# Nine r·k tiles transposed by DMA, smaller load groups and a new instruction order in an RWKV-6 plus mixture-of-adapters kernel

## The chip, the cores and the metric

One core of a Trainium2 chip runs the whole kernel. The metric is the device time of one execution in microseconds (us). Three runs of the kernel before gave 92.51, 93.12 and 93.5 us, so the median is 93.12 us.

## What is computed

The inputs are r, k, v, w of shape (4, 8, 768, 48), that is 4 batches, 8 heads, 768 steps and 48 channels. A linear-attention recurrence runs over the steps, and its output goes through a top-2 mixture of eight rank-16 adapters:

```python
for t in range(S):                       # attention, per batch and head
    y[t]  = r[t] @ (state + (u * k[t]) v[t]^T)
    state = w[t][:, None] * state + k[t] v[t]^T
x = y as (B*S, H*D)                      # 3072 rows of 384
logits = x @ w_gate                      # 8 experts, top 2, softmax over these two
out = x + sum over the two of  weight * ((x @ A[e]) @ B[e])
```

## The kernel before

**Tiling.** The 3072 rows are 24 tiles of 128 rows (6 tiles to a batch), and each tile is 128 rows by 384 columns (8 heads of 48). All steps of a tile t are small functions named `step(t)`, written `step.t` in the order list.

**Steps of one tile.** `load_w`, `load_rk`, `load_v` bring the inputs in: w by SyncE's (SP's) hardware DMA queue, r, k and v by GpSimd's (POOL's) software queue, which casts to 16 bits on the way. `ln` takes the logarithm of w for two tiles on ScalarE (ACT). `cs` and `ci` sum it up along the rows by matmuls, and `grow` and `exps` take exponentials of that on ACT. `mult` scales r and k with them (VectorE, DVE), `tr` transposes both on TensorE (PE), `trev` copies the result out of PSUM, `amm` multiplies r with k, `aev` masks the product on DVE, `kv` and `sev` update the state, `ymm` makes y. The diagonal term with u needs r·k: `rkp` multiplies r and k elementwise (POOL or DVE) into the half of a buffer that `mult` of the tile before has just read, so `rkp.t` waits for `mult.(t-1)`. `xk.(t)` then transposes in one PSUM tile both the finished rows `xs` of tile t (three 128x128 blocks) and the r·k of tile t+3 (`LEAD` = 3, three more blocks). `xkev` copies the six blocks to SBUF. From the r·k blocks `dgmm` makes the diagonal factors (three tiny matmuls), `dgev` copies those of two tiles, `dv` multiplies them with v on POOL, and `xev` adds them to y on DVE: `xs`.

**Adapters.** `lgmm`, `gate`, `gmax`, `gsel`, `gmul` make the gate in batches of (4, 4, 4, 4, 4, 3, 1) tiles; `zmm`, `zw`, `zT`, `zTev` the low-rank part; `dmm` its second product; `oev` adds x and leaves the output rows in `res`, either on DVE, or on ACT with one extra PE matmul by the identity that adds x in PSUM; `store` issues the output on SP.

**What sets the order.** A written-out list `ORDER` names every step once. Each engine executes its own steps in the sequence of this list, and waits on semaphores where it needs another engine or a DMA. Two steps on different engines are not tied to each other by their place in the list. The strings in `ENGINES` choose the engine for each tile (A for ACT, D for DVE, P for POOL). Each DMA waits, besides its data, for the landing of the DMA eight before it on its queue.

Lines that matter below: L174 `load_w`, L192 `load_rk`, L200 `load_v`, L337 `mult`, L345 `rkp`, L350 `dgmm`, L362 `dv`, L390 `tr`, L414 `aev`, L458 `xev`, L467 the transposes of `xk`, L273 copies on ACT (`trev`, `xkev`, `zTev`), L282 `ln`, L480 `lgmm`, L524 `zmm`, L572 and L573 `dmm` (identity matmul and product), L591 and L593 `oev` on ACT and on DVE, L600 `store`.

Of the kernel before, what the change touches and what calls it, by code (L numbers as in the profile page):

```python
# [37 lines left out]
ORDER = """
warm.0 warm.1 csc.0 warm.2 warm.3 warm.4 load_w1.0 warm.5 load_v.0 ln.0 load_rk.2 load_rk.3 load_v.2 cs.0 rkp.0 ci.0
xk.-3 grow.0 multr.0 exps.0 xkev.-3 trr.0 ln1.0 trevr.0 load_w.2 masks.0 load_rkf.1 load_wsb.0 mult.0 adapters.0  # L40
load_rk.4 load_w.4 tr.0 trev.0 pad.0 cs.1 amm.0 load_w.6 grow.1 ci.1 exps.1 load_rk.6 load_w.8 aev.0 kv.0 load_v.4
sev.0 ln.2 pad.1 cs.2 grow.2 rkp.1 load_rk.8 mult.1 xk.-2 xkev.-2 rkp.2 ci.2 load_v.8 tr.1 exps.2 cs.3 kv.1 cast16.0
mult.2 load_rk.12 grow.3 trev.1 dgmm.0 dgmm.1 dgev.1 sev.1 ymm.0 rkp.3 casts.0 amm.1 load_v.12 load_w.10 tr.2 ci.3
aev.1 trev.2 exps.3 kv.2 dv.0 amm.2 ymm.1 sev.2 xev.0 xk.-1 dv.1 ln.4 load_rk.16 mult.3 tr.3 xkev.-1 xev.1 kv.3 cs.4
trev.3 aev.2 load_v.16 xk.0 grow.4 dgmm.2 pad.2 ci.4 xkev.0 sev.3 rkp.4 amm.3 dgmm.3 load_w.12 exps.4 mult.4 xk.1
rkp.5 dgev.3 dv.2 dv.3 xkev.1 load_v.20 cs.5 ymm.2 lgmm.0 dgmm.4 aev.3 grow.5 xev.2 lgmm.1 tr.4 ci.5 ln.6 exps.5
ymm.3 trev.4 cs.6 xk.2 amm.4 mult.5 rkp.6 xev.3 xkev.2 grow.6 ci.6 xk.3 tr.5 dgmm.5 lgmm.2 ln.8 exps.6 trev.5 cs.7
xkev.3 grow.7 aev.4 lgmm.3 dgmm.6 zmm.3 ci.7 amm.5 gate.3 mult.6 rkp.7 tr.6 gmax.3 ln.10 dgev.5 dv.4 exps.7 aev.5
kv.4 cs.8 load_rk.20 gsel.3 mult.7 gmul.3 ymm.4 trev.6 sev.4 grow.8 amm.6 ci.8 xev.4 kv.6 ln.12 dv.5 exps.8 tr.7
sev.6 xk.4 trev.7 cs.9 zw.3 zT.3 ymm.5 kv.7 xkev.4 aev.6 lgmm.4 zTev.3 dmm.0 dmm.1 grow.9 ci.9 xev.5 dmm.2 mult.8  # L50
sev.7 oev.0 dgmm.7 rkp.8 amm.7 load_w.14 exps.9 cs.10 oev.1 dgev.7 tr.8 ymm.6 dv.6 oev.2 grow.10 xk.5 ln.14 dv.7
ci.10 exps.10 aev.7 xev.6 store.0 kv.8 ymm.7 rkp.9 trev.8 cs.11 xk.6 mult.9 sev.8 xkev.5 amm.8 kv.9 tr.9 lgmm.5
grow.11 xkev.6 load_w.16 mult.10 ci.11 dmm.3 dgmm.8 rkp.10 xev.7 aev.8 dgmm.9 lgmm.6 xk.7 trev.9 exps.11 dgev.9
sev.9 amm.9 cs.12 xkev.7 oev.3 rkp.11 tr.10 grow.12 aev.9 load_w.18 ymm.8 mult.11 trev.10 ci.12 lgmm.7 dgmm.10 dv.8
xev.8 gate.7 exps.12 ymm.9 kv.10 sev.10 dv.9 amm.10 tr.11 gmax.7 xk.8 ln.16 xkev.8 rkp.12 mult.12 cs.13 rkp.13
grow.13 gsel.7 xev.9 zmm.7 gmul.7 dgmm.11 lgmm.8 store.1 ci.13 xk.9 trev.11 exps.13 tr.12 xkev.9 aev.10 cs.14
dgev.11 trev.12 zw.7 grow.14 amm.11 zT.7 ymm.10 kv.12 mult.13 load_w.20 store.2 load_w.22 dgmm.12 ci.14 aev.11 dv.10
zTev.7 ln.18 dmm.4 ymm.11 exps.14 xev.10 xk.10 xkev.10 lgmm.9 cs.15 dv.11 sev.12 oev.4 xev.11 grow.15 amm.12 dmm.5
dgmm.13 dgev.13 rkp.14 tr.13 lgmm.10 dmm.6 mult.14 xk.11 aev.12 rkp.15 oev.5 dmm.7 trev.13 ci.15 xkev.11 amm.13
# [4 lines left out]
rkp.17 trev.16 xkev.13 oev.8 mult.17 amm.16 exps.18 sev.16 store.5 dmm.9 xk.14 cs.19 mult.18 oev.9 tr.17 rkp.18
xkev.14 ymm.15 grow.19 dgmm.16 ci.19 trev.17 dmm.10 exps.19 dgmm.17 tr.18 lgmm.13 aev.16 cs.20 kv.18 amm.17 xev.15
trev.18 rkp.19 grow.20 dgev.17 sev.18 xk.15 mult.19 ci.20 xkev.15 rkp.20 oev.10 aev.17 exps.20 dv.16 tr.19 ymm.16
lgmm.14 lgmm.15 cs.21 trev.19 xev.16 kv.19 gate.15 mult.20 grow.21 gmax.15 amm.18 xk.16 xkev.16 aev.18 dgmm.18 dv.17
dmm.11 oev.11 ci.21 exps.21 ymm.17 gsel.15 dgmm.19 sev.19 dgev.19 mult.21 zmm.15 cs.22 amm.19 kv.20 ymm.18 grow.22
sev.20 rkp.21 store.6 xev.17 gmul.15 ci.22 dv.18 store.7 xk.17 exps.22 xkev.17 zw.15 aev.19 tr.20 zT.15 xev.18 cs.23
lgmm.16 mult.22 dgmm.20 lgmm.17 trev.20 zTev.15 amm.20 dmm.12 grow.23 ci.23 xk.18 oev.12 aev.20 rkp.22 tr.21 dmm.13  # L70
store.8 store.9 ymm.19 xkev.18 trev.21 dgmm.21 exps.23 dgev.21 oev.13 dmm.14 amm.21 dv.19 tr.22 oev.14 xev.19 xk.19
xkev.19 mult.23 ymm.20 dmm.15 lgmm.18 lgmm.19 rkp.23 dv.20 aev.21 dgmm.22 trev.22 dv.21 ymm.21 tr.23 amm.22 gate.19
oev.15 store.10 trev.23 kv.21 xev.20 xk.20 gmax.19 zmm.19 xev.21 xk.21 sev.21 xkev.20 xkev.21 dgmm.23 gsel.19 aev.22
dgev.23 gmul.19 zw.19 dv.22 amm.23 kv.22 zT.19 ymm.22 store.11 sev.22 kv.23 lgmm.20 dv.23 lgmm.21 zTev.19 dmm.16
aev.23 xev.22 xk.22 oev.16 ymm.23 xev.23 xkev.22 lgmm.22 dmm.17 dmm.18 gate.22 zmm.22 oev.17 oev.18 gmax.22 xk.23
gsel.22 dmm.19 xkev.23 gmul.22 lgmm.23 zw.22 zmm.23 zT.22 oev.19 gate.23 store.12 zTev.22 gmax.23 dmm.20 gsel.23
zw.23 dmm.21 oev.20 oev.21 store.13 dmm.22 zT.23 store.14 zTev.23 oev.22 store.15 dmm.23 store.16 oev.23 store.17
store.18 store.19 store.20 store.21 store.22 oeva.23 store.23 storea.23
# [59 lines left out]
def kernel(  # L138
# [317 lines left out]
    def xev(t):  # L456
# [2 lines left out]
                             st[t]["y_ps"].rearrange("p a b -> p (a b)"))  # L459
        st[t]["xs"] = xs  # L460

    def xk(t):
        xk_ps = pp.tile([128, 6, 128], FP16, name="xk_ps", **slot("xk", t))
        for q, src in enumerate((st[t]["xs"] if t >= 0 else None, st[t + LEAD]["rkp"] if t + LEAD < NT else None)):
            if src is not None:
                for j in range(3):
                    nc.tensor.transpose(xk_ps[:, 3 * q + j, :], src[:, j * 128:(j + 1) * 128], ident16)  # L467
# [191 lines left out]
```

## Time and profile before

| | |
|---|---|
| runs | 92.51, 93.12, 93.5 us |
| profiled execution, time | 93.14 us |
| profiled execution, span from first to last instruction | 91.4 us |
| mean granted TensorE clock | 0.994 |
| ACT busy | 69.0 us (75%) |
| POOL busy | 50.3 us (55%) |
| software DMA queue (r, k, v) | 6.69 MB, 43.0% of 16 engines' span |
| hardware DMA queue of SP | 10.55 MB, 35.5% |

The span is what the profile sees; 1.7 us of the execution lie around it. The slices cut the span into 40 parts of 2.3 us, each digit being the busy share in tenths. A matmul is charged from its start to a modelled end, and matmuls overlap, so the distance between the starts of two neighbours tells what one costs the engine.

### The profile page before, as it was taken

The numbers are of one execution on the slowest core, as the hardware profiler recorded it, in microseconds if no ns is written. First come the engines' busy times: TensorE is split into PE (matmuls) and PEld (weight loads), VectorE is DVE, ScalarE is ACT, GpSimd is POOL, SyncE is SP. The second block draws the span as 40 slices with busy tenths as digits, with TensorE's granted clock in tenths as the row PEclk, the third lists the DMA queues.
The fourth block names the chain that finished last, engine by engine and source line by source line (L and its number), as shares of the span: only waits on it lengthen the run. The fifth ranks groups of instructions, "written<-read, shape, count | busy, mean of one in ns | idle before, by whom it ended". The sixth has DMA issues, their size and how long they took to land.

```text
span 91.4 us, 3313 instructions
## 1 busy us (share of the span) xinstructions
PE 79.3 (87%) x1335; PEld 59.1 (65%) x1335; DVE 76.9 (84%) x165; ACT 69.0 (75%) x164; POOL 50.3 (55%) x77
## 2 busy tenths in 40 slices
PE   5978868997999999999599999999999999979510
PEld 2435336875776867887467788787778878955200
DVE  5612898989999799999589999999999999976830
ACT  5237659998799979993998999998889868628210
POOL 6999357358029834976175833954649752532000
PEclk9999999999999999999999999999999999999997
DMA  1999999999999999999999999322201043105481
GB/s 29 317 215 266 267 272 261 261 264 275 274 249 217 208 213 204 245 260 263 272 277 273 262 254 266 103 86 86 93 31 55 7 173 126 55 4 186 159 296 48
DMA packets 13599, 17.53 MB, mean 192 GB/s; under 512 B 912, under 2 KB 13328, under 8 KB 13584
## 3 DMA queue, kind: packets, MB, share of 16 engines
q0 software_dynamic: 6128, 6.69, 43.0%
q1 hardware_dynamic: 7312, 10.55, 35.5%
q8 instruction: 10, 0.16, 0.7%
q10 hardware_dynamic: 144, 0.10, 0.3%
q14 instruction: 5, 0.04, 0.1%
HBM read 19.29 MB, written 4.72 MB: 263 GB/s over the span
## 4 chain that ended last, share of the span: by engine, by line
PE 47%; DMA 19%; DVE 14%; ACT 8%; issue 4%; SPq 2%; ACTq 0%; DVEq 0%
DMA w_in<-in_w_dram 10%; DMA rk_first<-in_rk_dram 9%; PE trp L390 8%; PE xk_ps L467 6%; PE a_ps L408 5%; DVE at L414 5%; PE d_ps L573 3%; PE y_ps L452 3%; PE z_ps L524 3%; DVE rk L337 3%; PE cs_ps L316 3%; PE s_ps L425 3%; DVE xs L458 2%; PE cs_ps L304 2%; PE cs_ps L305 2%
## 5 line engine op out<-in xcount | busy, mean ns | idle before, releaser
L414 DVE TENSOR_TENSOR at<-a_ps,strict 128x1024 f16<-128x1024 f32 x24 | 29.2, 1216 | 2.2 <-PE a_ps L408 2.2
L362 POOL TENSOR_TENSOR dv<-v,dg 128x384 f32<-128x384 f16 x24 | 20.2, 859 | 10.4 <-ACT dg L267 10.2
L345 POOL TENSOR_TENSOR e<-rk 128x384 f16<-128x384 f16 x15 | 14.0, 935 | 12.2 <-DVE rk L337 9.6
L309 ACT ACTIVATE e<-cs_ps 128x384 bf16<-128x384 f32 x24 | 11.9, 497 | 4.5 <-PE cs_ps L305 4.4
L273 ACT COPY rkT<-trp 128x512 f32<-128x512 f32 (+1 forms) x23 | 13.3, 578 | 1.7 <-PE trp L390 1.4
L390 PE MATMUL trp<-ident,rk 128*128 128x128 bf16 x184 | 14.1, 219 | 0.4 <-DVE rk L337 0.4
L458 DVE TENSOR_TENSOR xs<-dv,y_ps 128x384 f16<-128x384 f32 x24 | 13.1, 546 | 0.9 <-PE y_ps L452 0.4
L337 DVE TENSOR_TENSOR rk<-rk,e 128x768 bf16<-128x768 f16 x22 | 12.0, 554 | 1.4 <-ACT e L320 1.4
L273 ACT COPY xkT<-xk_ps 128x384 f32<-128x384 f32 (+1 forms) x23 | 10.3, 449 | 3.5 <-PE xk_ps L467 3.2
L320 ACT ACTIVATE e<-cs_ps 128x384 bf16<-128x384 f32 x23 | 11.4, 495 | 1.0 <-PE cs_ps L316 1.0
L390 PEld LDWEIGHTS <-rk 128*128 128x128 bf16 x184 | 10.9, 98 | 1.9 <-DVE rk L337 0.8
L282 ACT ACTIVATE logw<-w_in 128x768 f16<-128x768 f32 x11 | 9.3, 846 | 1.5 <-DMA w_in<-in_w_dram 1.5
L408 PE MATMUL a_ps<-rkT 48*128 48x128 bf16 x192 | 9.5, 218 | 0.6 <-DVE at L414 0.4
L267 ACT CAST S_sb<-s_ps 128x384 bf16<-128x384 f32 x19 | 9.3, 487 | 0.6 <-PE s_ps L425 0.4
L452 PE MATMUL y_ps<-v,at 128*128 128x48 f16 x192 | 8.7, 183 | 0.7 <-DVE at L414 0.7
L467 PE MATMUL xk_ps<-ident,xs 128*128 128x128 f16 x72 | 8.0, 219 | 0.7 <-DVE xs L458 0.6
L408 PEld LDWEIGHTS <-rkT 48*128 48x128 bf16 x192 | 5.7, 94 | 3.8 <-ACT rkT L273 1.3
L467 PE MATMUL xk_ps<-ident,e 128*128 128x128 f16 x69 | 7.6, 219 | 0.5 <-DVE e L345 0.5
L305 PE MATMUL cs_ps<-logw,strict 128*128 128x384 f16 x24 | 7.8, 325 | 0.0
L316 PE MATMUL cs_ps<-logw,ident 128*128 128x384 f16 x23 | 7.5, 326 | 0.3 <-ACT e L309 0.2
L452 PEld LDWEIGHTS <-at 128*128 128x128 f16 x192 | 7.0, 96 | 1.0 <-DVE at L414 0.8
L593 DVE TENSOR_TENSOR res<-d_ps,xs 128x384 f32<-128x384 f32 x14 | 7.4, 552 | 0.1
(100 smaller groups left out, 159.4 us busy)
## 6 DMA issues: line engine op xcount, KB each, us to landing
out_dram<-res SPq DMA_DIRECT2D x23, 192.0 KB, 2.0
w_in<-in_w_dram SPq DMA_DIRECT2D x11, 384.0 KB, 13.9
rk<-in_rk_dram POOLq DMA_DIRECT2D x4, 768.0 KB, 27.5
v<-in_v_dram POOLq DMA_DIRECT2D x5, 384.0 KB, 26.5
rk_first<-in_rk_dram SPq DMA_DIRECT2D x2, 384.0 KB, 5.9
rk<-in_rk_dram POOLq DMA_DIRECT2D x2, 384.0 KB, 13.1
w_in<-in_w_dram SPq DMA_DIRECT2D x2, 192.0 KB, 3.9
v<-in_v_dram POOLq DMA_DIRECT2D x2, 192.0 KB, 9.6
```

What stands on the lines that cost most here:

```text
L273: nc.scalar.copy(out=out.bitcast(F32), in_=in_.bitcast(F32))
L309: nc.scalar.activation(out=e2[:, 0], in_=cs_ps[:, 0:HD], func=ACT.Exp)
L320: nc.scalar.activation(out=st[t]["e2"][:, 1], in_=st[0]["c0"] if t == 0 else cs_ps[:, 0:HD], func=ACT.Exp, scale=-1.0)
L337: nc.vector.tensor_mul(rk2.rearrange("s m p h d -> s (m p h) d")[:, :, 0:D], st[t]["rk"].rearrange("s m (h d) -> s (m h) d", d=D), st[t][" ...
L345: (nc.gpsimd if ENGINES["rkp"][t] == "P" else nc.vector).tensor_mul(p_, st[t]["rk"][:, 0], st[t]["rk"][:, 1])
L362: nc.gpsimd.tensor_mul(dv_, st[t]["v16"], st[t]["dg"].rearrange("p (h o) -> p h o", o=1).to_broadcast([L, H, D]))
L390: nc.tensor.transpose(trp[:, m, p, :], rk2[:, m, p, :, :].rearrange("s a b -> s (a b)"), ident)
L408: nc.tensor.matmul(a_ps[:, g, p, :], lhsT=rkT[base:base + D, 1, p, :], rhs=rkT[base:base + D, 0, p, :], start=True, stop=True)
L414: nc.vector.tensor_mul(at, st[t]["a_ps"].rearrange("s g p f -> s (g p) f"), strict.rearrange("s (o f) -> s o f", o=1).to_broadcast([128, H ...
L452: nc.tensor.matmul(y_ps[:, h, :], lhsT=d["at"][:, g * P + p, :], rhs=d["v16"][:, h, :], start=(c == 0 and h == 0), stop=(h == H - 1), skip ...
L458: nc.vector.tensor_add(xs, st[t]["dv"].rearrange("p a b -> p (a b)"), st[t]["y_ps"].rearrange("p a b -> p (a b)"))
L467: nc.tensor.transpose(xk_ps[:, 3 * q + j, :], src[:, j * 128:(j + 1) * 128], ident16)
```

## The change

The r·k of tiles 15 to 23 is no longer transposed by `xk` but by a new step `dr`: one DMA transpose, issued by SP, from the SBUF buffer that `rkp` wrote to an SBUF buffer that `dgmm` reads. `xk` and `xkev` of tiles 12 to 20 handle three blocks and not six. (`dx`, the same for `xs`, exists but is used for no tile.) v of tiles 4 to 7, and r and k of tiles 8 to 11, come in groups of two tiles where they came in groups of four. Some steps change their engine, and the whole of `ORDER` is new.

```diff
-VGROUPS = {0: 2, 2: 2, 4: 4, 8: 4, 12: 4, 16: 4, 20: 4}
-VBUFS = {2: 2, 4: 5}
-RKGROUPS = {2: 1, 3: 1, 4: 2, 6: 2, 8: 4, 12: 4, 16: 4, 20: 4}
-RKBUFS = {1: 2, 2: 2, 4: 4}
+VGROUPS = {0: 2, 2: 2, 4: 2, 6: 2, 8: 4, 12: 4, 16: 4, 20: 4}
+VBUFS = {2: 4, 4: 4}
+RKGROUPS = {2: 1, 3: 1, 4: 2, 6: 2, 8: 2, 10: 2, 12: 4, 16: 4, 20: 4}
+RKBUFS = {1: 2, 2: 4, 4: 3}
...
-    trev="ADAAAAAAAAAAAAAAAAAAAAAA",
-    xkev="ADADADDAAAAAAAAAAAAAAAAAAAA",
-    out="DDADDADDDDDAADAADAAADDDA",
-    sev="DAAAAAAAAAAAAAAAAAAAAAAA",
-    rkp="PDDDDDDPPDPPPPPPPPPPDPPP",
-    dgev="AAAAAAAAADAAAAAAAAAAAAAA",
-    zTev="DDDADDDADDDDDDDADDDADDAA",
+    trev="DDAAAAAAAAAAAAAAAAAAAAAA",
+    xkev="AAADADAADAAAAAAAAAAAAAAAAAA",
+    out="DDADDADDDADAADAAAAAADAAA",
+    sev="DADADAAAAAAAAAAAAAAAAAAA",
+    rkp="DDDDPDPPPPPPPPPPPPPPDPPP",
+    dgev="ADADAAADADAAADAAAAAAAAAA",
+    zTev="DDDADDDADDDDDDDADDDADDAD",
...
+DX = ()
+DR = tuple(range(15, 24))
...
+    def parts(t):
+        return (t if 0 <= t and t not in DX else None, t + LEAD if t + LEAD < NT and t + LEAD not in DR else None)
+
     def xk(t):
+        x, r = parts(t)
         xk_ps = pp.tile([128, 6, 128], FP16, name="xk_ps", **slot("xk", t))
-        for q, src in enumerate((st[t]["xs"] if t >= 0 else None, st[t + LEAD]["rkp"] if t + LEAD < NT else None)):
+        for q, src in enumerate((None if x is None else st[x]["xs"], None if r is None else st[r]["rkp"])):
...
+    def dr(t):
+        sb = wk.tile([128, 3, 128], FP16, name="rD", bufs=6)
+        nc.sync.dma_start_transpose(out=sb, in_=st[t]["rkp"])
+        st[t]["rkpT"] = sb
```

The part of the old and of the new list around tile 15:

```diff
-exps.15 kv.13 oev.6 oev.7 sev.13 tr.14 trev.14 cs.16 ymm.12 dv.12 aev.13 mult.15 grow.16 lgmm.11 store.3 kv.14
-gate.11 amm.14 ln.20 dv.13 xev.12 rkp.16 tr.15 xk.12 ci.16 sev.14 exps.16 ymm.13 zmm.11 cs.17 gmax.11 xkev.12
-gsel.11 dgmm.14 dgmm.15 kv.15 aev.14 gmul.11 trev.15 amm.15 grow.17 dgev.15 ci.17 zw.11 dv.14 mult.16 sev.15 xev.13
+aev.13 rkp.15 cs.16 trev.14 lgmm.9 load_w.22 lgmm.10 dgmm.14 lgmm.11 kv.14 dv.12 amm.14 grow.16 mult.15 ci.16 dv.13
+dr.15 xev.12 tr.15 gate.11 sev.14 dgmm.15 zmm.11 gmax.11 exps.16 cs.17 xk.12 ymm.13 rkp.16 gsel.11 gmul.11 ln.20
+trev.15 xkev.12 kv.15 aev.14 grow.17 amm.15 sev.15 dgev.15 zw.11 ci.17 zT.11 lgmm.12 dr.16 exps.17 ln.22 mult.16
```

The sequence on SP, where nothing overtakes:

| before | after |
|---|---|
| w of tiles 0, 1, 2; rk of 0, 1; weights, B; w of tiles 4 to 15 (six DMAs) | the same, and w of 16 (seven DMAs) |
| store.0, w.16, w.18, store.1, w.20, store.2, w.22 | store.0, store.1, w.18, w.20, w.22 |
| store.3 to store.22, store.23 | dr.15, dr.16, store.2, dr.17, dr.18, dr.19, store.3, dr.20, store.4, store.5, dr.21, store.6, dr.22, dr.23 |
| | store.7 to store.22, store.23 |

More of the change, by code (lines that the diff above doesn't have):

```diff
@@ L38 @@
 ORDER = """
[L39 to L58, printed above, removed]
@@ L64 @@
[L64 to L78, printed above, removed]
+csc.0 warm.0 warm.1 warm.2 warm.3 warm.4 warm.5 load_v.0 ln.0 load_rk.2 load_w1.0 load_rk.3 load_w.2 rkp.0 load_v.2
@@ new lines @@
+ymm.15 ci.19 lgmm.14 dmm.10 aev.16 trev.17 dr.17 dgmm.17 xev.15 tr.18 exps.19 cs.20 xk.15 sev.16 kv.18 trev.18
+oev.10 rkp.19 mult.19 grow.20 amm.17 tr.19 ci.20 dgev.17 sev.18 ymm.16 xkev.15 dv.16 dr.18 rkp.20 exps.20 lgmm.15
+kv.19 dmm.11 gate.15 cs.21 aev.17 trev.19 ymm.17 dgmm.18 oev.11 xev.16 xk.16 grow.21 gmax.15 mult.20 dv.17 gsel.15
+amm.18 ci.21 dr.19 tr.20 rkp.21 sev.19 store.3 xev.17 xkev.16 xk.17 exps.21 trev.20 dgmm.19 aev.18 xkev.17 dgev.19
+mult.21 zmm.15 gmul.15 cs.22 zw.15 lgmm.16 dv.18 amm.19 kv.20 rkp.22 lgmm.17 grow.22 aev.19 ci.22 exps.22 tr.21
@@ new lines @@
+zT.15 ymm.18 cs.23 trev.21 amm.20 zTev.15 dmm.12 mult.22 sev.20 grow.23 dmm.13 oev.12 tr.22 ci.23 xev.18 dr.20
+store.4 exps.23 store.5 dr.21 rkp.23 ymm.19 dgmm.20 dgmm.21 xk.18 trev.22 xkev.18 dv.19 aev.20 store.6 dr.22 oev.13
+amm.21 dgev.21 xev.19 dmm.14 dv.20 xk.19 dr.23 oev.14 mult.23 ymm.20 dgmm.22 dv.21 lgmm.18 xkev.19 aev.21 dgmm.23
+dmm.15 lgmm.19 xev.20 gate.19 dgev.23 oev.15 tr.23 ymm.21 xk.20 gmax.19 trev.23 amm.22 xkev.20 store.7 xev.21 kv.21
+sev.21 xk.21 dv.22 zmm.19 xkev.21 lgmm.20 gsel.19 gmul.19 kv.22 aev.22 dv.23 amm.23 zw.19 zT.19 ymm.22 sev.22
@@ L107, in runs @@
         return t < len(WARM)
+    if f == "dx":
+        return t in DX
+    if f == "dr":
+        return t in DR
+    if f in ("xk", "xkev"):
+        return 0 <= t and t not in DX or t + LEAD < NTILE and t + LEAD not in DR
     if f == "pad":
```

45 lines of the change are left out of this document (38 added, 7 removed).

## The prediction

> **What bounds the kernel now.** I read the slices first, then a table of stretches, then the waits.
>
> ```profile
> span 91.4 us, 3313 instructions
> PE 79.3 (87%) x1335; PEld 59.1 (65%) x1335; DVE 76.9 (84%) x165; ACT 69.0 (75%) x164; POOL 50.3 (55%) x77
> ...
> PE   5978868997999999999599999999999999979510
> DVE  5612898989999799999589999999999999976830
> DMA  1999999999999999999999999322201043105481
> ```
>
> ```profile
> core 0: us, PE busy (x) PEld busy (x) DVE busy (x) ACT busy (x) POOL busy (x), PEclk, DMA share, GB/s
> 43.00:46.00 3.00, 1.81 (x30) 1.39 (x27) 1.88 (x3) 2.81 (x7) 0.75 (x3) 1.00 1.18 273
> 58.00:62.00 4.00, 4.00 (x76) 3.14 (x75) 4.00 (x7) 3.95 (x10) 2.87 (x4) 1.00 0.20 67
> 62.00:75.00 13.00, 13.00 (x245) 10.26 (x243) 12.90 (x27) 10.85 (x28) 8.05 (x11) 1.00 0.19 66
> ```
>
> Three things stand out. From slice 20 on (46 us) PE and DVE are both full: in 62 to 75 us PE is busy for 13.00 and DVE for 12.90 of 13 us. Work taken from only one of them would gain little; work taken from both shortens the stretch by the smaller of the two. Second, the DMA engines are saturated until slice 26 (59 us) and nearly idle after. Third, there is one hole, at 43 to 46 us, where PE and DVE each lose 1.1 to 1.2 us. The list of waits names its cause, and SP's timeline shows why:
>
> ```profile
> ACT logw L282 <- DMA w_in<-in_w_dram: 1.5, 1, 1.5
> ```
>
> ```profile
> 4.12 9.09 SPq L174 DMA_DIRECT2D w_in<-in_w_dram  x6
> 33.62 0.36 SPq L600 DMA_DIRECT2D out_dram<-res  x1
> 34.02 1.11 SPq L174 DMA_DIRECT2D w_in<-in_w_dram  x2
> ```
>
> Six w loads are issued by 13.2 us. The seventh, w of tile 16, stands behind store.0, so it goes out at 34.02 us, into saturated DMA engines. ACT's `ln` for tile 16 then waits 1.5 us, and everything queued behind it on ACT waits too. PE's next transposed tile comes from there.
>
> **The change, part by part.**
>
> *w of tile 16 ahead of store.0.* SP issues it as the seventh of the batch, once the DMA eight before it (the weights) has landed, so at some 13 us instead of 34. `ln.16` then has its data long before 43 us. Next late could be `ln.18`, whose load now follows store.1 directly, no later than before; nothing else in that hole waits for a DMA. The wait is 1.5 us on ACT, but the two full engines lost less. I take 1.1 us (PE: 3.00 - 1.81 = 1.19; DVE: 3.00 - 1.88 = 1.12). The early load takes DMA time from r, k and v; only the one wait above on an input shows after the start, so I charge nothing and keep a rival for it.
>
> *Transposes leave PE, copies on ACT get narrower.*
>
> ```profile
> 58.46 0.33 PE L467 MATMUL xk_ps<-ident,xs 128*128 128x128 f16 x3
> 58.62 0.33 PE L467 MATMUL xk_ps<-ident,e 128*128 128x128 f16 x3
> 58.79 0.33 PE L573 MATMUL d_ps<-Ball,zT 128*128 128x384 f16 x1
> 58.95 0.33 PE L316 MATMUL cs_ps<-logw,ident 128*128 128x384 f16 x1
> ```
>
> Three r·k transposes hold PE from 58.62 to 58.79, 0.17 us; nine tiles make 1.5 us. One 128x384 matmul holds it from 58.79 to 58.95, 0.16 us.
>
> ```profile
> L273 ACT COPY xkT<-xk_ps 128x384 f32<-128x384 f32 x18 | 8.7, 484 | 1.6 <-PE xk_ps L467 1.5
> L273 ACT COPY xkT<-xk_ps 128x192 f32<-128x192 f32 x5 | 1.6, 323 | 1.9 <-PE xk_ps L467 1.7
> L591 ACT COPY res<-d_ps 128x384 f32<-128x384 f32 x9 | 4.2, 482 | 0.5 <-PE d_ps L573 0.4
> ```
>
> On ACT nine copies shrink from 484 to 323 ns, 1.4 us less.
>
> *`oev` of tiles 9, 16, 21 and 22 moves from DVE to ACT.* Each gives PE an identity matmul of 0.16 us and ACT a copy of 482 ns, and frees DVE for one slot:
>
> ```profile
> 60.86 0.55 DVE L593 TENSOR_TENSOR res<-d_ps,xs 128x384 f32<-128x384 f32 x1
> 61.32 1.22 DVE L414 TENSOR_TENSOR at<-a_ps,strict 128x1024 f16<-128x1024 f32 x1
> ```
>
> A slot is 61.32 - 60.86 = 0.46 us. Tiles 9 and 16 fall into the full stretch, 21 and 22 into the tail. So DVE gets 0.92 us shorter there, less about 0.1 us for `dgev.13`, which moves to it. PE gets 1.5 - 2 x 0.16 = 1.2 us shorter. The smaller one counts: 0.8 to 0.9 us; I take 0.9. ACT's balance, 4 x 0.48 more and 1.4 less, is covered by its idle 2.15 us in 62 to 75.
>
> *Early engine moves.* DVE hands `rkp` of tiles 4, 6 and 9 to POOL, which is 55% busy, and takes `rkp.0`, two `sev`, four `dgev` and one `trev`. These nearly cancel; zero, with 0.3 us either way. The smaller load groups let tiles 6, 7, 10 and 11 start without waiting for a group of four; the trace shows no wait on r, k or v there, so zero as well.
>
> *The tail.* With `oev` of 21 and 22 on ACT the last three output tiles no longer queue on DVE, but zT.23 still needs the PSUM buffer that `oev.20` frees. Zero.
>
> *What the DMA transposes add.* Each moves 128 x 384 x 2 B = 96 KB, off PE. The price is latency, since `dgmm.t` sits in PE's fixed sequence, and if the transpose hasn't landed all of PE waits, and DVE soon after. So I need the time from the end of `rkp.t` to `dgmm.t`. The tightest three:
>
> ```profile
> 49.82 0.91 POOL L345 TENSOR_TENSOR e<-rk 128x384 f16<-128x384 f16 x1 [1.11 <-DVE rk L337]
> 53.72 0.62 PE L390 MATMUL trp<-ident,rk 128*128 128x128 bf16 x8
> 54.18 0.33 PE L467 MATMUL xk_ps<-ident,xs 128*128 128x128 f16 x3
> 58.58 0.91 POOL L345 TENSOR_TENSOR e<-rk 128x384 f16<-128x384 f16 x1
> 61.67 0.32 PE L573 MATMUL d_ps<-Ball,zT 128*128 128x384 f16 x1
> 72.12 0.91 POOL L345 TENSOR_TENSOR e<-rk 128x384 f16<-128x384 f16 x1 [0.50 <-DVE rk L337]
> 75.29 0.32 PE L572 MATMUL d_ps<-xs,ident 128*128 128x384 f16 x1
> ```
>
> Tile 15: `rkp.15` ends at 50.73. In the new list `dgmm.15` follows `tr.15` at once, so it would come at 54.18, plus some 0.25 us for `ci.16`, `dgmm.14` and an `lgmm` that moved ahead of it. That leaves 3.7 us. Tile 17: `rkp.17` now runs before `dv.15`, one `dv` earlier than here, so it ends near 58.7; `dgmm.17` follows `dmm.10`, at about 61.83 less two freed groups of transposes (0.33): 2.8 us. Tile 23: from 73.03 to `dmm.15` at 75.29, 2.3 us. Earlier gains shift both ends alike.
>
> No row shows a DMA transpose. The nearest are SP's stores: one issued at 33.62, when SP's queue was empty but the loads streamed, and seven issued after the loads had ended.
>
> ```profile
> L600 SPq DMA_DIRECT2D out_dram<-res x1: 361/361/361, 33.6 to 33.6; - x1
> ...
> DMA to landing us min/median/max: 5.8/5.8/5.8
> ```
>
> ```profile
> out_dram<-res SPq DMA_DIRECT2D x7, 192.0 KB, 1.9
> ```
>
> Quiet, 1.9 us is enough for all three. But dr.15 goes out at about 49.5 us (50.73 less the 1.1 gained), inside the load stream. That ends earlier than before, since six stores move behind the transposes: by the lines above a quiet 192 KB store needs at most 1.9 us, so an upper bound is 6 x 1.9 = 11 us; at the 273 GB/s of the 43 to 46 us row their 1.2 MB are 4.4 us, so it ends near 55 us rather than 59. Its landing is bounded by 1.9 and 5.8 us. If half the bytes pay half of the excess it is 3.9, if they pay all of it 5.8; I take the middle, 4.85, nearer to the row of the saturated stretch. `dgmm.15` is then late by 4.85 - 3.7 = 1.15 us, with a range of 0.2 to 2.1. dr.16 comes some 4 us later, when the stream is about to end, and needs no charge. For tiles 17 to 23 I take the quiet row: no charge.
>
> *Queued behind.* On SP store.2 waits behind dr.15 and dr.16, and sixteen stores behind dr.23 (about 73 us less the gains). `res` has twelve buffers, so store.2 is first missed by `oev.14`, twelve tiles on; up to the last store 14 us remain for sixteen issues of some 0.36 us each. No charge; without these buffers `oev` would stall. POOL's `rkp` reuses a buffer that a transpose reads only six tiles later.
>
> *Sum* on the profiled execution's 93.14 us (span 91.4, 1.7 around it; median of the runs 93.12): 93.14 - 1.1 - 0.9 + 1.15 = 92.3 us. The case's own range is 91.3 to 93.3.
>
> **The rivals.**
>
> *No transposition is late.* DMA transposes are few and small beside the stream, or the stream ends sooner. For it: half the bytes of a store. Against it: the 5.8 us row. Then 93.14 - 2.0 = 91.1 us, and 90.6 if the early moves give their 0.3 and the tail a little.
>
> *Transposition is slow even in quiet (slower than before).* A transpose writes two-byte pieces across partitions, which no store does, so 1.9 us may not hold. At the middle between 1.9 and 5.8, 3.85 us, `dgmm.17` is late by 1.05 and `dgmm.23` by 1.55 us, with 1.15 at tile 15: 93.14 - 2.0 + 3.75 = 94.9 us. It decides from about 3.0 us on, where 0.2 + 0.7 + 1.15 eat up the gain of 2.0. For it: the margins are thin, nothing in the trace vouches for a short transpose, and PE and DVE have no slack to absorb a stall. Against it: the quiet DMA engines.
>
> On this the Trainium skill has two views. "VectorE: DVE Perf Modes", section "The three transpose paths", gives 1309 ns for a 128x128 block by DMA against 390 ns on TensorE and says to use TensorE where a PSUM result will do, as it does here; three blocks one after another would be an estimated 3.9 us, which is this rival. "Advanced Engine Details and Errata", section "X-Bar Transpose (TRN2)", says that transposing DMAs are as fast as regular ones, by which the quiet stores' row would hold and the sum stays at 92.3. No run shown so far can tell.
>
> *The hole at 43 us stays.* The early w load pushes r and k of tiles 12 to 15 back, and `rkp.12` or `mult.12` waits in its place: 92.3 + 1.1 = 93.4 us. Against it: no input but this w was waited for.
>
> **How the numbers follow.** The forecast has 0.40, no late transposition 0.25, slow transposition 0.27, the hole that stays 0.08. "Same" means within 1%, 92.2 to 94.1, about what a measurement of this kernel can tell from no change. Faster: 0.24 from the first rival and 0.18 from the forecast's lower half, 0.42. Slower: 0.27 from the slow transposes, and 0.04 from the edges of the other cases, 0.31. Same: 0.27. The range 90.6 to 95.0 leaves out the fastest fifth of the first rival (0.05) and the slow transposes with more than 3.9 us (0.13). The forecast alone has 91.3 to 93.3.
>
> **What would show it.** No wait of `ln` on w near 43 us, and no hole of PE there; transposes by PE 27 fewer, ACT's narrow copies nine more; a wait of PE's L359 (`dgmm`) on the DMA of `rD`, once, of about 1 us, near 53 us. Several such waits, or quiet landings over 3 us, mean the slow rival; none means the first. The forecast is wrong if a new wait on r, k or v appears before 46 us.

## The result, and the profile after

The changed kernel took 98.72 us (median of four runs, 97.54 to 99.73), the kernel before, run beside it, 93.31 us (92.51 to 94.93): a ratio of 1.052 with an interval of 1.036 to 1.067. The prediction was 92.3 us, with a range from 90.6 to 95.0. Here and in the experiments the medians take in every run, while the ratios leave out the runs of each kernel that were slower than its others, most of them at a lower clock. The profiled execution of after took 97.54 us with a span of 95.8, against 93.14 and 91.4: 4.4 us more.

From the page of after, span and slices:

```profile
span 95.8 us, 3283 instructions
...
PE   3988899996889999999999209999999987997610
...
DVE  5625989989998999999999703699999996975610
...
PEclk9999999999999999999999985999999999999996
DMA  1999999999999999999999912010446429915390
```

Two things are new in the slices. PE drops to 2 and 0 in slices 23 and 24 (52.7 to 57.5 us), and DVE follows. The row PEclk, the granted clock, has a dent right behind, 8 and 5. The DMA row confirms that the load stream now ends at about 55 us.

The list of waits of after names the new hole (us in total, times, longest):

```profile
PE s_ps L359 <- DMA rD<-e: 4.9, 2, 4.0
```

L359 is `dgmm`. It waited twice for a transposition, once for 4.0 us. The chain of work that ended last, in order of time (start, length), says when, and for which tiles:

```profile
49.47 7.79 DMA rD<-e
57.30 0.24 PE s_ps L359 x3
...
76.09 3.44 DMA rD<-e
79.58 0.23 PE s_ps L359 x3
```

The first is `dr.15`, issued at 49.47 us and landed 7.8 us later, the second `dr.23`, landed after 3.4 us. The landings of the instructions on `rD`, all nine together, show that these are not the rule (shortest, median, longest):

```profile
DMA to landing us min/median/max: 2.3/2.3/7.8
```

The table of stretches of after (columns as in the prediction) holds the old hole and the new one:

```profile
42.00:46.00 4.00, 4.00 (x74) 3.55 (x71) 4.00 (x8) 3.77 (x11) 2.27 (x5) 1.00 1.15 266
...
53.00:57.40 4.40, 0.44 (x10) 0.27 (x8) 1.53 (x4) 1.64 (x3) 0.68 (x3) 0.92 0.59 89
57.40:61.00 3.60, 3.60 (x49) 3.07 (x50) 1.71 (x3) 1.00 (x3) 0.00 (x0) 0.62 0.15 55
```

From 42 to 46 us PE and DVE are now full, where they lost over 1 us before. From 53 to 57.4 us PE does 0.44 us of work in 4.4. Then it is busy for all of 3.6 us, but at a granted clock of 0.62.

To see where the 4.4 us come from, take one step that every tile has, the masking `aev` on DVE, and compare its starts in the two timelines. The distance between two starts is what that stretch costs.

| stretch | before, us | after, us | difference | predicted |
|---|---|---|---|---|
| start to tile 10 | 42.80 | 43.11 | +0.31 | 0 |
| tile 10 to 11 (the hole at 43 us) | 3.85 | 2.20 | -1.65 | -1.1 |
| tile 11 to 14 | 8.08 | 8.04 | -0.04 | 0 |
| tile 14 to 15 (`dr.15`) | 3.13 | 8.46 | +5.33 | +1.15 |
| tile 15 to 21 | 16.67 | 16.18 | -0.49 | -0.9 |
| tile 21 to 22 (`dr.23`) | 2.98 | 3.74 | +0.76 | 0 |
| tile 22 to the end | 13.89 | 14.07 | +0.18 | 0 |
| sum | 91.4 | 95.8 | +4.4 | -0.85 |

One stretch carries the result, and of its 5.33 us 3.96 are the wait itself (shown below in PE's timeline). Four questions are left: what the rest of the 5.33 us is, why one transposition took 7.8 us where most took 2.3, why `dr.23` was late in quiet, and what the relief of PE and DVE was worth.

### The profile page after: what moved, and what is told of

Same layout as the page of the kernel before. It is cut to its first block, busy times and chain, and to the rows that moved or that the text cites. A ratio compares the mean times of both kernels' runs of the same rounds, so it can differ in the third digit from the quotient of the medians.

```text
span 95.8 us, 3283 instructions
## 1 busy us (share of the span) xinstructions
PE 80.1 (84%) x1312; PEld 59.6 (62%) x1312; DVE 76.6 (80%) x166; ACT 67.6 (71%) x161; POOL 53.2 (56%) x81
## 4 chain that ended last, share of the span: by engine, by line
PE 50%; DVE 16%; DMA 12%; issue 6%; ACT 5%; POOL 5%; POOLq 0%; DVEq 0%; ACTq 0%
DMA rD<-e 12%; PE trp L399 6%; DVE at L423 5%; PE a_ps L417 4%; POOL e L354 4%; PE a_ps L262 4%; PE xk_ps L480 4%; PE y_ps L461 3%; PE cs_ps L325 3%; PE cs_ps L314 3%; PE z_ps L549 3%; PE s_ps L434 3%; PE cs_ps L313 3%; PE d_ps L598 2%; DVE rk L346 2%
## 5 line engine op out<-in xcount | busy, mean ns | idle before, releaser
L354 POOL TENSOR_TENSOR e<-rk 128x384 f16<-128x384 f16 x18 | 16.8, 936 | 8.3 <-DVE rk L346 7.1
L282 ACT COPY xkT<-xk_ps 128x192 f32<-128x192 f32 (+1 forms) x24 | 9.3, 388 | 5.6 <-PE xk_ps L480 5.4
L276 ACT CAST S_sb<-s_ps 128x384 bf16<-128x384 f32 x17 | 8.2, 484 | 1.9 <-PE s_ps L434 1.1
L564 DVE TENSOR_TENSOR zw<-z_ps,g 128x512 f16<-128x512 f32 (+1 forms) x6 | 4.0, 666 | 5.3 <-PE z_ps L549 4.4
L201 POOL DMA_DIRECT2D rk<-in_rk_dram x9 | 6.3, 707 | 2.5 <-DMA v<-in_v_dram 1.7
L616 ACT COPY res<-d_ps 128x384 f32<-128x384 f32 x13 | 6.2, 484 | 1.9 <-PE d_ps L598 1.9
```

The source lines that it names most:

```text
L282: nc.scalar.copy(out=out.bitcast(F32), in_=in_.bitcast(F32))
L354: (nc.gpsimd if ENGINES["rkp"][t] == "P" else nc.vector).tensor_mul(p_, st[t]["rk"][:, 0], st[t]["rk"][:, 1])
```

## The experiments

Ratios are to the kernel before, run on the same chip in the same batch. "From tile 14 to tile 21" and the like is the distance between the starts of these tiles' masking steps.

### Tile 15

**Only tile 15 back on TensorE.**

```diff
-DR = tuple(range(15, 24))
+DR = (16, 17, 18, 19, 20, 21, 22, 23)
...
-dv.13 dr.15 xev.12 tr.15 gate.11 sev.14 dgmm.15 zmm.11
+dv.13 xev.12 tr.15 gate.11 sev.14 zmm.11
...
-trev.15 xkev.12 kv.15
+trev.15 xkev.12 dgmm.15 kv.15
```

> The changed kernel with tile 15 transposed by TensorE again (xk of tile 12 takes six blocks, dgmm.15 stands behind xkev.12); tiles 16 to 23 stay on DMA. In the changed kernel the transposition of tile 15 took 7.8 us to land, TensorE waited 3.96 us for it, and then ran for some 3.5 us at a lower granted clock; at the masking steps the kernel was 1.4 us ahead of the one before at tile 14 and 4.0 us behind at tile 15. Theory A, the loads: the loss is this one wait and the slow clock behind it. Then 97.5 - 5.3 = 92.2 us, with up to 0.5 us for tile 16, which is still issued into the last loads. Theory B, the transposes or the new order cost time everywhere: at least 96 us.

Measured: 92.51 us, ratio 0.994 [0.987, 1.001], close to the 92.2 expected. The 4 us wait is gone, none comes at tile 16 in its place, and the clock has no dent. One transposition put back on TensorE removes the whole loss. `dr.16`, issued at 53.9 us at the end of the stream, landed in 2.7 us. What is left is a wait of 1.5 us for tile 23, looked at below.

**Tiles 15 and 16 back on TensorE.** As above, and:

```diff
-DR = tuple(range(15, 24))
+DR = (17, 18, 19, 20, 21, 22, 23)
...
-lgmm.12 dr.16 exps.17
+lgmm.12 exps.17
...
-dmm.8 dgmm.16 grow.18
+dmm.8 grow.18
...
-rkp.17 xkev.13 kv.16
+rkp.17 xkev.13 dgmm.16 kv.16
```

> The changed kernel with tiles 15 and 16 transposed by TensorE; 17 to 23 stay on DMA, all issued after the loads. A: no wait of TensorE on a transposition before the last tile's (0.9 us in the changed kernel), clock 0.99, 91.5 to 92 us, 0.2 to 0.5 below the run with only tile 15 moved if tile 16 was late too, equal to it if not. B: at least 96 us.

Measured: 93.77 us, ratio 1.005 [0.999, 1.012], and not the 91.5 to 92 expected. There was nothing to win at tile 16. From tile 14 to tile 21 this order takes 20.48 us (before 19.80, with only tile 15 on TensorE 19.75). Most of the difference lies between tiles 16 and 17 (3.61 us against 3.04 with only tile 15), where `dgmm.16` now stands behind `xkev.13`.

**The stream ends earlier.** Tiles 20 to 23 read the r, k and v that tiles 16 to 19 loaded.

```diff
     def load_rk(t):
+        if t == 20:
+            for i in range(n):
+                st[t + i]["rk"] = st[t + i - 4]["rk"]
+            return
...
     def load_v(t):
+        if t == 20:
+            for i in range(n):
+                st[t + i]["v16"] = st[t + i - 4]["v16"]
+            return
```

> The changed kernel without the loads of r, k and v of tiles 20 to 23: these tiles compute with the data of tiles 16 to 19, everything else is unchanged. The loads then end at some 45 us, before tile 15's transposition goes out. Theory A, the load stream holds it up: it lands in 2.3 to 2.7 us like the quiet ones, TensorE doesn't wait for it, the granted clock stays at 0.99, and the time is 97.5 - 5.3 = about 92 us. Rival: the first transposition, or one issued behind many w loads on its own queue, is slow by itself: it still takes over 4 us.

Measured: 93.42 us, ratio 0.998 [0.994, 1.002]. The long wait is gone: tile 15 starts 0.54 us ahead of before where tile 14 was 0.69 ahead. The 92 us expected were not reached. Tile 23 waits 1.4 us here, so that tile 21 to 22 takes 4.25 us in place of 2.98, and this execution was 1.0 us behind before by tile 10. `dr.15` alone, among the instructions on `rD` (duration on SP in ns; then its time to landing in us):

```profile
L508 SPq DMA_TRANSPOSE rD<-e x1: 1293/1293/1293, 50.2 to 50.2; - x1
...
DMA to landing us min/median/max: 3.9/3.9/3.9
```

So without the end of the load stream the landing is 7.8 - 3.9 = 3.9 us shorter. The 3.9 us that stay are more than the 2.3 of quiet, so a second cause is there; the section on tile 23 shows it.

What makes the landing in the stream 7.8 us, longer than the 5.8 of a whole store of before, is only partly shown. Stretches of 1 us of after, ahead of the landing at 57.3:

```profile
54.00:55.00 1.00, 0.00 (x0) 0.00 (x0) 0.57 (x1) 0.64 (x2) 0.15 (x1) 1.00 0.95 132
55.00:56.00 1.00, 0.00 (x0) 0.00 (x0) 0.00 (x0) 0.00 (x0) 0.00 (x0) 1.00 0.36 57
56.00:57.00 1.00, 0.00 (x0) 0.00 (x0) 0.00 (x0) 0.00 (x0) 0.00 (x0) 0.85 0.12 18
```

At 55 us most of the stream is over; the DMA share drops from 0.95 to 0.36 and 0.12. For two more microseconds every engine of the core stands still, and most DMA engines too: from 56.3 us on only packets of the transposition are left, which keep hardly more than one of the sixteen engines busy (8.1% of them over 1 us). In the kernel of the next experiment the same transposition took 9.0 us, and there the last load packet ended at 57.7 us. This points at the few DMA engines that finish last with the loads; the trace does not name them. In after an instruction fetch (section on tile 23) ran in the same stretch; DMA queues from 53 to 54 us, the share being that of 16 engines:

```profile
q8 instruction: 1, 0.02, 15.7%
```

That is 2.5 us of one engine. Why some engines finish so much later than the rest, and how much of the 7.8 us is this fetch, is not settled.

**PE kept busy while it waits.** Sixty matmuls on zeros, which add nothing, ahead of `dgmm.15`.

```diff
+    def busy(t):
+        for _ in range(60):
+            nc.tensor.matmul(cs_ps[:, HD:512], lhsT=zeros, rhs=zeros, start=False, stop=True, skip_group_check=True)
...
-gate.11 sev.14 dgmm.15
+gate.11 sev.14 busy.15 dgmm.15
```

> The changed kernel with 60 extra matmuls of zeros (128 columns, an unused part of a PSUM bank) right ahead of dgmm.15, about 3.3 us of TensorE work put inside the 4.0 us wait. If the clock drops because TensorE stood idle, it stays near 1.0 now and the 1.4 us lost to it come back: about 96.2 us against 97.5 to 98.2. If the drop has another cause, or the matmuls make the wait longer, there is no gain.

Measured: 95.72 us, ratio 1.024 [1.017, 1.031], better than after's 1.052. PE's timeline (start, length, what ran, in brackets the wait), this kernel first, then after:

```profile
52.85 3.51 PE L268 MATMUL cs_ps<-zeros 128*128 128x128 f16 x60
58.19 0.23 PE L362 MATMUL s_ps<-w,rD 128*128 128x8 f16 x3 [1.83 <-DMA rD<-e]
58.28 0.83 PE L552 MATMUL z_ps<-w,xkT 128*128 128x128 f16 x12
```

```profile
52.74 0.61 PE L399 MATMUL trp<-ident,rk 128*128 128x128 bf16 x8
57.30 0.24 PE L359 MATMUL s_ps<-w,rD 128*128 128x8 f16 x3 [3.96 <-DMA rD<-e]
57.41 1.44 PE L549 MATMUL z_ps<-w,xkT 128*128 128x128 f16 x12
```

The transposition was later still, 58.19 against 57.30. But the clock stays full, and the twelve matmuls behind `dgmm.15` take 0.83 us and not 1.44. From `dgmm.15` to the start of tile 15's masking it is 3.22 us here (58.19 to 61.41), and 4.51 us in after (57.30 to 61.81). So the lowered clock cost 1.29 us. With the 3.96 us of the wait that makes 5.25 of the 5.33 us.

### Tile 23

`dr.23` landed after 3.4 us in after and after 4.0 in the kernel with tile 15 on TensorE, long after the loads had ended.

**Stores moved ahead.** If the stores that queue behind the transposition on SP slowed it, moving them should change it. To the kernel with tile 15 on TensorE:

```diff
-tr.17 grow.19 store.2 ymm.15
+tr.17 grow.19 ymm.15
...
-ci.21 dr.19 tr.20 rkp.21 sev.19 store.3 xev.17
+ci.21 dr.19 store.2 store.3 store.4 store.5 store.6 tr.20 rkp.21 sev.19 xev.17
...
-dr.20 store.4 exps.23 store.5 dr.21
+dr.20 store.7 store.8 store.9 store.10 exps.23 dr.21
...
-aev.20 store.6 dr.22
+aev.20 dr.22
...
-dr.23 oev.14
+dr.23 store.11 store.12 store.13 oev.14 store.14
```

(store.15 to store.22 then each follow their `oev`.)

> The kernel with only tile 15 moved back to TensorE, with SP's stores placed otherwise: stores 2 to 6 behind the transposition of tile 19, 7 to 10 behind that of tile 20, the others behind that of tile 23 and only as they become ready. In three profiles a transposition with two or more ready stores right behind it landed in 3.4 to 4.2 us, all other quiet ones in 2.3 to 2.7; TensorE waited 1.5 us for tile 23. Theory: it is those stores. Then tile 23 lands in about 2.3 us, tile 19 in about 4 (it has room), the wait goes and the time falls from 92.5 to about 91.2 us. Rival: the last transposition is late for another reason (GpSimd hands over late, TensorE needs it early): it still waits about 1.5 us, 92.5 us.

Measured: 95.31 us, ratio 1.007 [1.002, 1.012]. This theory fell: `dr.19`, with five stores of 192 KB right behind it, landed in 2.3 us and not in some 4, and `dr.23` still took 3.3 us, with three waits on `rD`, 2.0 us in all. What the slow landings do share is an instruction fetch. The profile's table of DMA queues has a queue "q8 instruction", 16 KB at a time, about every 7 us. From the issue of `dr.23` on, in after and in the kernel with tile 15 on TensorE:

```profile
q8 instruction: 1, 0.02, 1.8%
issues: line engine op xcount, KB each, median us to landing
...
rD<-e SPq DMA_TRANSPOSE x1, 3.4
```

```profile
q8 instruction: 1, 0.02, 1.5%
issues: line engine op xcount, KB each, median us to landing
...
rD<-e SPq DMA_TRANSPOSE x1, 4.0
```

The share is of 16 engines over a window of some 4 us, so 1.8% is 1.2 us of one engine. A transposition with nothing else in flight keeps nearly all sixteen busy at once (the tenths of `dr.18` in the kernel with tile 15 on TensorE, 61.5 to 63.9 us), so one engine that is held up can make it late:

```profile
DMA  0000000000000000000026999998420100000000
```

Over the ten kernels with transpositions by DMA, 65 of them were issued after 57 us. Without a fetch in flight between issue and landing there are 38, and 37 of them landed after 2.3 or 2.4 us, one after 2.7. With a fetch there are 27, from 2.3 to 4.2 us, 19 of them 3.0 or more.

**The fetch shifted.** Sixty matmuls of eight columns on zeros, in the first 13 us, where PE waits anyway. They change no other instruction, only how many lie before each place in PE's program. To the kernel with tile 15 on TensorE:

```diff
+    def busy(t):
+        for _ in range(30):
+            nc.tensor.matmul(cs_ps[:, HD:HD + 8], lhsT=zeros, rhs=zeros[:, 0:8], start=False, stop=True,
+                             skip_group_check=True)
...
-xk.-3 exps.0 trr.0
+xk.-3 exps.0 busy.0 trr.0
...
-rkp.1 load_w.6 cs.2
+rkp.1 load_w.6 busy.1 cs.2
```

> The kernel with only tile 15 moved back to TensorE, plus 60 tiny matmuls of zeros (8 columns each, an unused part of a PSUM bank) in TensorE's idle time before 12 us, 30 ahead of tile 0's transposes and 30 ahead of cs.2. In the profiles so far SP's DMAs that were in flight with one of the 16 KB instruction fetches (q8, every 7 us or so) landed 1 to 2 us later than the rest, and tile 23's transposition met one in all kernels but one: the one with the extra matmuls, where the fetches stood elsewhere. The stores behind it are ruled out as the cause, since tile 19's with five stores behind it landed in 2.3 us. Theory: the fetch follows the count of TensorE's instructions; 120 more of them move it some 3 us forward, tile 23's transposition lands in 2.3 us, TensorE doesn't wait for it, and the time falls by 1.3 us to some 91.2 us. Rival: the lateness belongs to tile 23's place; TensorE still waits 1.5 us and the time stays at 92.5 us or above it.

Measured: 92.61 us, ratio 0.986 [0.981, 0.990]; without the shift it was 92.51 us, 0.994 [0.987, 1.001]. The intervals overlap and the median did not fall, so the times do not show the gain that was expected (some 91.2 us); the timeline does: from tile 21 to 22 it takes 2.89 us in place of 4.33. The fetches came at 63, 70 and 76 us in place of 66, 73 and 80. `dr.23`, in the same table of this kernel, lands without one in its time:

```profile
q1 hardware_dynamic: 771, 0.18, 39.3%
issues: line engine op xcount, KB each, median us to landing
...
rD<-e SPq DMA_TRANSPOSE x1, 2.3
```

No wait on `rD` is left at all. The slow ones after the loads are now those issued at 62.1 us (3.9), 63.3 (3.5) and 68.8 (3.8), next to the fetches at 63 and 70; their places in the order have the room. The same list of steps with the same stores thus has another late transposition. That the fetch is PE's own is inferred from what moved it; the profile does not name its reader.

**Tile 23 on TensorE too.** To the kernel with tile 15 on TensorE:

```diff
-DR = (16, 17, 18, 19, 20, 21, 22, 23)
+DR = (16, 17, 18, 19, 20, 21, 22)
...
-xk.19 dr.23 oev.14
+xk.19 oev.14
...
-aev.21 dgmm.23 dmm.15 lgmm.19 xev.20 gate.19 dgev.23 oev.15
+aev.21 dmm.15 lgmm.19 xev.20 gate.19 oev.15
...
-amm.22 xkev.20 store.7
+amm.22 xkev.20 dgmm.23 dgev.23 store.7
```

> The changed kernel with tiles 15 and 23 transposed by TensorE (dgmm.23 behind xkev.20, dgev.23 behind it), 16 to 22 by DMA. Tile 23's wait of 1.5 us goes, three transposes and a wider copy come back on the path at the end (0.3 us), and dgmm.23 stands later: 91.5 us, if the late tile 23 is all that is left. If dgmm.23 comes too late for the steps behind it, it stays at 92.5 us.

Measured: 92.59 us, ratio 0.991 [0.988, 0.995], where 91.5 us was expected. No wait on `rD`, but tile 23's masking comes 2.63 us after tile 22's, against 1.73 in before and 1.76 with the fetch shifted: `dgmm.23` now stands behind `xkev.20`. These 0.9 us are about what the fetch cost in after.

### The hole at 43 us

**The kernel before, with w of tile 16 ahead of store.0 and nothing else.**

```diff
-amm.7 load_w.14 exps.9
+amm.7 load_w.14 load_w.16 exps.9
...
-grow.11 xkev.6 load_w.16 mult.10
+grow.11 xkev.6 mult.10
```

> The kernel before with one move: the w load of tiles 16 and 17 goes out ahead of store.0. If the hole at 43 us comes from this load alone, it closes and the time falls by 1.1 us (the idle time of TensorE) to 1.6 us (what the changed kernel gained between the masking steps of tiles 10 and 11): 91.5 to 92.0 us. If another load takes its place, it stays at 93.1 us.

Measured: 91.89 us, ratio 0.985 [0.980, 0.991], as expected if this load alone makes the hole. The stretch of the old hole in this kernel:

```profile
42.00:46.00 4.00, 4.00 (x70) 3.38 (x70) 3.90 (x9) 4.00 (x11) 2.34 (x5) 1.00 1.15 263
```

PE and DVE are full, and tile 10 to tile 11 takes 2.34 us in place of 3.85. So this one move is worth 1.5 us, and nothing waits in its place.

### The relief of PE and DVE

**No transposition by DMA in the new order.**

```diff
-DR = tuple(range(15, 24))
+DR = ()
```

with every `dr` out of the list, and `dgmm` of 15, 16, 21, 22 and 23 (and `dgev.23`) moved behind the `xkev` that they need.

> The changed kernel with all nine tiles on TensorE and no DMA transpose: what is left is the new order, the smaller groups, the early w load and the moved engines. If transposes by DMA in quiet relieve TensorE as forecast, this is 0.5 to 1.2 us slower than the run with tiles 15 and 16 on TensorE, some 92.3 to 92.8 us. If they bring nothing, both are equal. B, with the order to blame: 96 us or more here too.

Measured: 95.37 us, ratio 1.023 [1.017, 1.029], neither the 92.3 to 92.8 us expected nor the 96 of theory B. From tile 14 to tile 21 it takes 21.77 us, 2.0 more than before. This says that the new order depends on the transposes being gone, not what they are worth, because the old order does nearly the same work without these 2.0 us. So the next kernels measure it in the old order.

**The old order with transposes of tiles 18 to 22 by DMA.** To the kernel before with w of tile 16 moved, each `dr` placed right behind its `rkp`:

```diff
+DR = tuple(range(18, 23))
...
-rkp.18 xkev.14
+rkp.18 dr.18 xkev.14
...
-rkp.19 grow.20
+rkp.19 dr.19 grow.20
```

and so on to `dr.22`, with the diff's `parts`, `xk`, `xkev` and `dr`.

> The kernel before with the w load ahead of store.0 (91.9 us), and on top of it only the r*k of tiles 18 to 22 transposed by DMA; order, engines and load groups as before. These tiles have 4 us or more from r*k to use, so no wait is expected. TensorE is relieved by 5 x 0.17 = 0.85 us, ScalarE by 0.8, VectorE by nothing. If VectorE bounds the full stretch too, 91.6 to 91.9 us; if TensorE alone bounds it, 91.0 us.

Measured: 92.44 us, ratio 0.984 [0.978, 0.991], no wait on `rD`. It is not faster than with w moved alone, as expected if DVE bounds the stretch too.

**The same, and `oev` of 9, 16, 21 and 22 on ACT.**

```diff
-    out="DDADDADDDDDAADAADAAADDDA",
+    out="DDADDADDDADAADAAAAAADAAA",
```

> The kernel before with the early w load and tiles 18 to 22 transposed by DMA (no faster than with the early load alone), and now oev of tiles 9, 16, 21 and 22 on ScalarE as in the changed kernel. VectorE loses two slots of 0.46 us in the full stretch and two at the end, TensorE gains 0.16 us for each. If both engines bound the stretch together, the relief of TensorE now shows: 0.9 us less, about 91.0 us. If the stretch is set by something else, such as the fixed order across the engines, it stays at 91.9 us.

Measured: 91.63 us, ratio 0.979 [0.974, 0.984]. The 91.0 us expected if both engines bound the stretch were not reached.

**`oev` on ACT without any transposition by DMA.** The edit of `out` above, on the kernel before with w of tile 16 moved.

> The kernel before, with w of tile 16 ahead of store.0 and with the output step of tiles 9, 16, 21 and 22 on ACT, but no transposition by DMA. Theory A (only work taken from PE and DVE together shortens the full stretch): DVE is relieved by two steps of 0.46 us there, PE gets two matmuls of 0.16 us more, so the start of the masking step of tile 20 stays within 0.2 us of where w of tile 16 alone put it (1.0 us before the kernel before), and the time stays near the 0.985 of w of tile 16 alone. Theory B (DVE alone sets the stretch, the transpositions are worth nothing): the ratio is 0.979 or less, as with the transpositions, and the masking step of tile 20 starts 1.4 to 1.5 us before the kernel before.

Measured: 91.88 us, ratio 0.989 [0.983, 0.996], near the 0.985 of theory A.

The four intervals overlap, so the ratios don't tell these kernels apart. The timeline does, since distances in it repeat to 0.01 us where the same work is done; single starts do not (the last of these four was 1.4 us ahead by tile 14 already). With only w moved, DVE's masking step of tiles 14, 16 and 20 starts at 53.72, 60.31 and 70.95 us. The same three rows with the transposes added, with both, and with `oev` alone:

```profile
53.72 1.22 DVE L422 TENSOR_TENSOR at<-a_ps,strict 128x1024 f16<-128x1024 f32 x1
60.30 1.22 DVE L422 TENSOR_TENSOR at<-a_ps,strict 128x1024 f16<-128x1024 f32 x1
70.95 1.21 DVE L422 TENSOR_TENSOR at<-a_ps,strict 128x1024 f16<-128x1024 f32 x1
```

```profile
53.70 1.22 DVE L422 TENSOR_TENSOR at<-a_ps,strict 128x1024 f16<-128x1024 f32 x1
59.83 1.21 DVE L422 TENSOR_TENSOR at<-a_ps,strict 128x1024 f16<-128x1024 f32 x1
70.79 1.21 DVE L422 TENSOR_TENSOR at<-a_ps,strict 128x1024 f16<-128x1024 f32 x1
```

```profile
52.34 1.22 DVE L414 TENSOR_TENSOR at<-a_ps,strict 128x1024 f16<-128x1024 f32 x1
58.46 1.21 DVE L414 TENSOR_TENSOR at<-a_ps,strict 128x1024 f16<-128x1024 f32 x1
69.60 1.21 DVE L414 TENSOR_TENSOR at<-a_ps,strict 128x1024 f16<-128x1024 f32 x1
```

From tile 14 to 16 the four take 6.59, 6.58, 6.13 and 6.12 us: the step taken from DVE (`oev.9`) gives its 0.46 us at once. From tile 14 to 20 they take 17.23, 17.23, 17.09 and 17.26: by tile 20 nearly all of it is lost again. Transposes off PE alone bring nothing, the output step off DVE alone brings nothing, and both together 0.14 us. The stretch from tile 16 to 20 shows what bounds, with the transposes alone, with both, and with `oev` alone (columns as in the prediction):

```profile
60.30:70.95 10.65, 10.45 (x197) 7.90 (x195) 10.55 (x23) 8.77 (x25) 6.91 (x10) 1.00 0.29 75
59.83:70.79 10.96, 10.87 (x208) 8.54 (x207) 10.74 (x24) 9.36 (x26) 7.37 (x10) 1.00 0.28 73
58.46:69.60 11.14, 11.14 (x215) 8.82 (x214) 10.75 (x23) 9.81 (x25) 7.38 (x10) 1.00 0.20 72
```

With the transposes alone DVE stays nearly full and PE idles for 0.20 us; with `oev` alone PE is full and DVE idles for 0.39. After tile 20 the two kernels with transposes lose some 0.35 us more by tile 23. So the kernel before with only w of tile 16 moved, 0.985, has nearly all that is to be had here, and each of these four beats both kernels. Which of them is fastest isn't settled: even the two that lie farthest apart, 0.979 with both edits and 0.989 with `oev` alone, have intervals that touch.

## Why the prediction was wrong

**The failed step.** "Its landing is bounded by 1.9 and 5.8 us [...] I take the middle, 4.85", so that `dgmm.15` is "late by 4.85 - 3.7 = 1.15 us". The mechanism and the place were the predicted ones: the wait is at `dgmm.15`, on the transposition, inside the load stream, and all of PE stood behind it. The size was off in two terms:

- The landing took 7.8 us. The upper end came from one store early in the stream, and was taken as a bound though other stores of before that fell into the stream had taken up to 14.8 us. The four issued where `dr.15` was to go out, from 48.8 to 52.0 us, had taken 6.7 to 7.4; by them the lateness would have been 3.0 to 3.7 us. By the 7.8 and the 3.7 us of room it is 4.1, and 3.96 were measured. With the stream cut short the same transposition took 3.9.
- A wait was charged at its own length. This one cost 1.29 us more, since the granted clock fell while PE stood. No row of before showed that price: its hole of 1.1 us went at a clock of 1.00.

The row of these four stores, in before:

```profile
L600 SPq DMA_DIRECT2D out_dram<-res x4: 332/332/357, 48.8 to 52.0; - x4
...
DMA to landing us min/median/max: 6.7/7.1/7.4
```

Had these two terms been right (3.96 + 1.29 in place of 1.15), the sum would have been 96.4 us. The profiled execution took 97.5; the rest is for the most part tile 23 and the part of the relief that did not come.

**"For tiles 17 to 23 I take the quiet row: no charge."** Wrong at tile 23, right elsewhere. The landing in quiet is 2.3 us, 0.4 over the stores' 1.9 and just the 2.3 us of room. With an instruction fetch in its time it is 3.4, and tile 23 waited 0.90 us. The quiet row was also read as a bound ("needs at most 1.9 us"), but 1.9 is the median of its seven stores. The longest took 2.8, issued at 72.5 us with a fetch in flight (L600 in before, 59 to 76 us):

```profile
L600 SPq DMA_DIRECT2D out_dram<-res x7: 332/332/657, 60.0 to 74.5; - x7
...
DMA to landing us min/median/max: 1.9/1.9/2.8
```

That a thin margin would fail was part of the slow rival; its cause was another.

**"dr.16 [...] needs no charge"** and the end of the stream "near 55 us rather than 59" held. `dr.16` took 4.4 us in after, but its tile had the room.

**The hole at 43 us.** Right, and undersized: -1.1 predicted, -1.65 in after, -1.51 by itself. The two engines lost 1.1 us inside 43 to 46 us, but DVE had a shortage behind it as well (0.64 us of work in the stretch from 46 to 47 us of before). The rival in which it stays is refuted.

**"Tiles 9 and 16 fall into the full stretch [...] PE gets 1.5 - 2 x 0.16 = 1.2 us shorter. The smaller one counts [...] I take 0.9."** Wrong, first by a reading of the timeline. In before `oev.16` runs at 81.10 us, behind the last masking step and the full stretch:

```profile
79.24 1.22 DVE L414 TENSOR_TENSOR at<-a_ps,strict 128x1024 f16<-128x1024 f32 x1
...
81.10 0.55 DVE L593 TENSOR_TENSOR res<-d_ps,xs 128x384 f32<-128x384 f32 x1
```

So in the full stretch only `oev.9` left DVE, and the smaller relief was one slot of 0.46 us (some 0.36 with `dgev.13`), not 0.9. The rule that work must be taken from both engines is borne out by the old order, where either relief alone gave nothing. Not all of the smaller relief came through: from tile 14 to 21 the kernel with the stream cut short, the only one with all nine transpositions and no long wait (and with fewer loads), gained 0.31 us (19.49 against 19.80), the one with tile 15 back on TensorE 0.05, and the old order 0.14 to tile 20. What the order of steps takes back, and how, is not shown step by step.

**The rivals.** "Transposition is slow even in quiet" is refuted as a mechanism: the median is 2.3 us for three blocks, below its point of decision at 3.0. Of the two pages of the Trainium skill that the prediction set against each other, "Advanced Engine Details and Errata", section "X-Bar Transpose (TRN2)", comes close: 2.3 us against 1.9 of a store. Three blocks at the 1309 ns of "VectorE: DVE Perf Modes", section "The three transpose paths", would be an estimated 3.9 us; in after the quiet landings with no instruction fetch beside them took 2.3. "No transposition is late" failed with `dr.15`.

**Nothing for the early moves, the load groups, the tail and the queued stores.** To tile 10 after came 0.31 us later, but the kernels that start as before does scatter there by more (-0.9 to +0.5 us, set within the first tiles), so no price can be read from it. The tail, with `oev` of 16, 21 and 22 off DVE, stayed within 0.2 us.

## What to carry to other kernels

A transfer that an engine's fixed sequence waits for has to be priced by the landings seen in the stretch where it is issued, and by the longest of them, not by a median or a middle. A wait that left PE idle for 3.4 us cost clock too. Where a change mixes a sure gain with a risky trade, try the sure part alone: one load moved up in its queue gave 1.5 us here, and the relief of two nearly full engines 0.1 to 0.3. Before adding up a relief, look up at what time each moved step runs: three of the four output steps moved here lay outside the full stretch. To see what it was worth, compare the distances between the starts of one recurring step in two timelines.
